# Moving block 0's first loads of the down product's weights in SyncE's queue

## The chip, the cores and the metric

The kernel runs on one core of one Trainium2 chip. A core has five engines that run side by side, each through its own queue of instructions in order: TensorE (PE: matrix products, with PEld for the loading of its stationary operand), VectorE (DVE), ScalarE (ACT), GpSimd (POOL) and SyncE (SP). SyncE computes nothing: it issues DMA transfers, which 16 DMA engines carry out. An instruction that has to wait holds up everything behind it in the queue of its engine. Intermediate results lie in the on-chip memory (SBUF) or in the banks of PSUM, where TensorE writes its products.

The metric is the time of one execution on the device, in microseconds (us): the median of several runs.

## The reference

One transformer block for 2048 rows of width 512, all in float32: a layer norm, attention with 32 heads of width 16 that share one key and one value, a residual, a second layer norm, a gated feed-forward product of inner width 1792, and another residual. Cut to what matters:

```python
q = (ln(x) @ wq) split into 32 heads of 16;  k = ln(x) @ wk;  v = ln(x) @ wv
p = softmax(q k^T / 4)
h = x + concat(p @ v) @ wo
out = h + (gelu(ln(h) @ w_gate) * (ln(h) @ w_up)) @ w_down
```

## The kernel before, in words

**Split numbers.** A product with float32 operands is made of three products of a faster format: an operand is split into a high and a low part (`split`), and high x high, high x low and low x high are summed. The weights of the feed-forward product are split once, by GpSimd (`part_weights`), and stored in two scratch tensors in HBM: `w1_d` (gate and up, 14 chunks of 128 columns) and `w2_d` (down, 14 chunks of 128 rows). From there they are loaded again for each block of rows: `load_w1` brings one chunk, 1 MB, into one of two buffers (L452), and `load_w2` brings two chunks, 1 MB, into one of three buffers (L457).

**Blocks and groups.** The 2048 rows are four blocks of 512 (b = 0 to 3). For a block, the heads are worked on in eight groups of four (g = 0 to 7), and for a group the 2048 keys in 16 chunks. For each chunk of keys TensorE makes the scores (L326), ScalarE takes the exponential (L330), and TensorE multiplies with the values and a column of ones and adds up in `acc` (L334). The loop counts half chunks: n runs through 256 of them for each block.

**The output of a group.** `evacuate` copies `acc` to `oT` (VectorE, L347), stores it to the scratch tensor `acc_d` (SyncE, L348) and reads it back in another arrangement into `oc` (four DMAs, L358). For each second group VectorE takes the reciprocals of the sums (L363), multiplies (L372) and splits the result into `o_hi` and `o_lo` (L108, L109).

**Two streams.** While the attention of block b + 1 runs, the rest of block b is computed between its pieces by the generator `dense(b)`: the product with wo (`pp`, L472), the residual with the input rows `xb` (loaded at L508, added at L535), the layer norm, the transposes (`pxt`, L543) into `x2h` and `x2l`, then for each of the 14 chunks f the products `pg` and `pu` (`up`), the gelu, and for each run of four chunks the product down (`down`, `pd`). `duo` (L472) makes two products at a time, each on one half of the rows of the array; between its two turns VectorE's one-column copies (L480) mark a bank as done. The last block's dense part has nothing beside it and runs as a tail.

**Who orders what.** The orders of TensorE, ScalarE and GpSimd are those of the program text everywhere (`manual_schedule`). Those of SyncE and VectorE are too, but only up to the end of the first part of the loop, the `while n < lead` loop, which ends three pieces of a group (16 half chunks) into block 1's attention. Behind it a planner in the framework orders SyncE and VectorE by its own estimate of when each instruction can run. It may also put one of these planned instructions between instructions of the written order, ahead of some that stand earlier in the text.

**Around the change.** At n = 256 the work on q and on the weights is finished, and the buffers of the dense part are opened in the place of theirs. At n = 260, within the written order, block 0's last group of heads is put out, and `dense(0)` is made and taken to its first `yield`: it issues the loads of `xb` for row tiles 0 and 1 and of the first two chunks of w1. The load of the next group's `qg` (L311) follows. The rest of `dense(0)` is taken in the planned part. In it the loads of w2 stand in the text in `for fs in RUNS`: the first two after the first `up`, the third and fourth behind the product down of the first run. `RUNS` is the 14 chunks as three runs of four and one of two.

Of the kernel before, what the change touches and what calls it, by code (L numbers as in the profile page):

```python
# [40 lines left out]
def kernel(  # L41
# [96 lines left out]
    def run(outer, first):  # L138
# [112 lines left out]
        def later_q():  # L251
            second = project_q(1, range(DC), nc.vector, 1)
            for _ in range(sum(RAMP.values())):
                yield next(second)

            next(q_rest)
            for _ in range(2 * DC - sum(RAMP.values())):
                yield next(second)
            yield from q_rest
            yield from second  # L260
            for b in range(2, NB):
                yield from project_q(b, range(DC), nc.vector, b)
            check_bound(eb, k2m)
# [77 lines left out]
        def take_out():  # L341
            for step in outs.pop(0):
                step()
# [106 lines left out]
        def load_w1(b, f):  # L450
            w = db.tile([P, 2, 2, DC, P], F32R, tag="w1", bufs=2, name=f"w1_{b}_{f}")
            nc.sync.dma_start(w.bitcast(F32), w1_d[f].bitcast(F32))  # L452
            return w[:, 0], w[:, 1]

        def load_w2(b, j):
            w = db.tile([P, 2, 2, D], F32R, tag="w2", bufs=3, name=f"w2_{b}_{j}")
            nc.sync.dma_start(  # L457
                w.bitcast(F32), w2_d[2 * j : 2 * j + 2].rearrange("f p i d -> p f i d").bitcast(F32)
            )
            return w[:, :, 0], w[:, :, 1]  # L460
# [38 lines left out]
        def dense(b, tail=False):  # L499
# [13 lines left out]
            xT_hi = db.tile([P, DC, T], F32R, tag="x2h", bufs=1, name=f"x2h_{b}")  # L513
            xT_lo = db.tile([P, DC, T], F32R, tag="x2l", bufs=1, name=f"x2l_{b}")
            w1 = {0: load_w1(b, 0), 1: load_w1(b, 1)}
            if b == 0:
                yield 0
            w2 = {}
            hs, xns, held = {}, {}, {}

            def project(t0):
# [94 lines left out]
            def up(f, gh, gl):  # L616
                hi, lo = w1.pop(f)
                terms = [
                    [
                        (wt[:, k, c, :], xt[:, c, :])  # L620
                        for c in range(DC)
                        for wt, xt in ((hi, xT_hi), (hi, xT_lo), (lo, xT_hi))
                    ]
                    for k in range(2)
                ]
                pg, pu = yield from product([f"pg_{b}_{f}", f"pu_{b}_{f}"], terms)
                g = db.tile([P, T], F32, tag="g", bufs=2, name=f"g_{b}_{f}")
                nc.vector.tensor_copy(g, pg)  # L628
                a = db.tile([P, T], F32, tag="ga", bufs=2, name=f"ga_{b}_{f}")
                nc.vector.tensor_tensor(a, g, g, op=ALU.mult)  # L630
                nc.vector.scalar_tensor_tensor(  # L631
                    a, a, 1.0 / GELU_A, g, op0=ALU.add, op1=ALU.mult
                )

                def gate():
                    nc.scalar.activation(a, a, AF.Tanh, scale=GELU_A * GELU_C)  # L636
                    nc.vector.scalar_tensor_tensor(a, a, 1.0, g, op0=ALU.add, op1=ALU.mult)
                    nc.vector.tensor_tensor(a, a, pu, op=ALU.mult)
                    split(nc.vector, gh[:, f % 2, :], gl[:, f % 2, :], a)

                gates.append(gate)
                if tail:
                    open_gates()
                yield CUT

            def down(fs, gs, last):
                tw = [w2.pop(f // 2) for f in fs[::2]]
                for t0 in range(0, TB, 2):  # L650
                    terms = []
                    for t in (t0, t0 + 1):
                        sl = slice(t * P, (t + 1) * P)
                        terms.append([
                            (gt[:, k, sl], wt[:, k, :])
                            for (gh, gl), (hi, lo) in zip(gs, tw)
                            for k in range(2)
                            for gt, wt in ((gh, hi), (gh, lo), (gl, hi))
                        ])
                    pds = yield from product(  # L660
                        [f"pd_{b}_{fs[0]}_{t0}", f"pd_{b}_{fs[0]}_{t0 + 1}"], terms
                    )
                    for t, pd in zip((t0, t0 + 1), pds):
                        nc.vector.tensor_tensor(hs[t], hs[t], pd, op=ALU.add)  # L664
                        if last:
                            nc.sync.dma_start(out_t[:, b * TB + t, :], hs[t])
                    yield CUT

            prev = None
            for fs in RUNS:  # L670

                early_f = 2 if fs is RUNS[-1] else 1
                gs = []
                for n, f in enumerate(fs):
                    if f % 2 == 0:
                        gs.append([
                            db.tile([P, 2, T], F32R, tag=tag, bufs=3, name=f"{tag}_{b}_{f}")
                            for tag in ("gh", "gl")
                        ])
                    yield from up(f, *gs[-1])  # L680
                    if f + 2 < FC:
                        w1[f + 2] = load_w1(b, f + 2)
                    if fs is RUNS[-1] and n == 0:
                        w2[f // 2] = load_w2(b, f // 2)
                    if n + 1 == early_f and prev is not None:
                        yield from down(*prev, False)
                    if fs is not RUNS[-1] and n + 1 == early_f:
                        for g in fs[::2]:
                            w2[g // 2] = load_w2(b, g // 2)
                prev = (fs, gs)  # L690
            yield from down(*prev, True)

# [19 lines left out]
        def drain():  # L712
            nonlocal work
            for _ in work or ():
                pass
            work = None
# [3 lines left out]
        def score(n):  # L720

            nonlocal acc
            i, u = divmod(n, 2)
            b, r = divmod(i, PER)
            g, kc = divmod(r, KC)
            if u == 0:
                if kc == 0:
                    cur["qg"] = qgs.pop((b, g))
                    acc = pss.tile([P, T], F32, tag="acc", bufs=1, name=f"acc_{b}_{g}")
                if kc == 2 and b * NG + g + 1 < NB * NG:  # L730
                    key = divmod(b * NG + g + 1, NG)
                    qgs[key] = load_q(*key)
                cur["p"] = sb.tile([P, 4, T], F32, tag="p", bufs=PB, name=f"p_{i}")
            scores(i, cur["p"], cur["qg"], kc, u)
            if u == 1:
                pend.append((b, g, kc, cur["p"], acc, n))
# [13 lines left out]
        with tc.manual_schedule(engines={mybir.EngineType.SP, mybir.EngineType.DVE}):  # L750
            parts = None
            if first:
                work = later_q()
                parts = part_weights(early.enter_context(tc.tile_pool(name="parts", bufs=1)))


            while n < lead:
                if n == 2 * PER:
                    drain()
                    for _ in parts or ():  # L760
                        pass
                    parts = None
                    early.close()
                    db = late.enter_context(tc.tile_pool(name="dense", bufs=1))
                if n % 4 == 0:
                    given = work is not None
                for _ in range(RAMP.get(n, n > 7 and n % 4 == 3) if given else 0):
                    if next(work, None) is None:
                        work = None
                score(n)  # L770
                n += 1
                if n % 4 == 2 and not given and len(pend) > 2:
                    finish(1)
                if n % 4:
                    continue
                if len(pend) > 2:
                    finish(len(pend) - 2)
                if outs:
                    take_out()
                if parts is not None and n > 12 and n % 24:  # L780
                    next(parts, None)
                if n == 2 * PER + 4:
                    primed = dense(0)
                    next(primed)
        assert not outs
        work = primed
        set_banks("ps_rest")
# [11 lines left out]
        for c in range(LEAD[0], (NB - 1) * NG * len(SIZES)):  # L799
            b, cb = divmod(c, NG * len(SIZES))  # L800
            cg = cb % len(SIZES)
            size, kind = SIZES[cg], None
            if b > 0 and cb == LEAD[b]:
                assert work is None
                work, todo = dense(b), list(kinds)
# [358 lines left out]
```

## Time and profile before

| | us |
|---|---|
| median of 3 runs | 1466.74 |
| lowest and highest | 1466.73, 1470.73 |
| the profiled execution | 1466.96 |
| its span, first to last instruction | 1465.2 |
| TensorE busy | 1417.1 |
| ScalarE busy | 1040.9 |
| VectorE busy | 533.3 |

The granted clock of TensorE was 0.997 of its full speed on average.

How to read the rows that follow. A row of a timeline has the start and the length in us, the engine, the line of the kernel, the operation, output and inputs by the program's names, and how many instructions were merged; a bracket tells how long the engine was idle ahead of it and what ended that. SPq is SyncE's queue; its DMA rows give the time that the issue took, not the transfer. A row of windows has the start and end of a stretch, its length, then the busy time of PE, PEld, DVE, ACT and POOL with the number of instructions, the granted clock, the mean busy share of the 16 DMA engines and the GB/s that they moved. A row of waits has the waiting engine and line, what it waited for, the sum, the number and the longest. A row of a tile has an instruction group's count, the shortest, median and longest duration in ns, and the starts of the first and the last in us.

### The profile page before, as it was taken

Reading aid. Unit: us, or ns where it says so; the run is one execution under the profiler, and the core shown is the slowest. Engines: PE = TensorE matmul, PEld = TensorE weight load, DVE = VectorE, ACT = ScalarE, POOL = GpSimd, SP = SyncE. Lnnn points to the kernel's source line nnn. Section 1 sums busy time; section 2 is a strip of 40 time slices with the busy share of each in tenths; the row PEclk is TensorE's granted clock in tenths of the full one; section 3 lists DMA queues with packets and bytes.
Section 4 is the critical chain, followed back from the end, with each engine's and each line's share of the span. In section 5 each row is a group of like instructions: output and inputs, shape, how many; then the busy total and the mean of one; then the engine's idle time right before and its main releaser. Section 6 shows DMA issues by size and latency. Waiting matters only on the chain.

```text
span 1465.2 us, 24785 instructions
## 1 busy us (share of the span) xinstructions
PE 1417.1 (97%) x10420; PEld 751.9 (51%) x10420; DVE 533.3 (36%) x920; ACT 1040.9 (71%) x1147; POOL 222.2 (15%) x301
## 2 busy tenths in 40 slices
PE   6999999999999999999999999999999999998998
PEld 5533333334555555554555555554555555556886
DVE  7413131213251424323251424324242423425665
ACT  7699999996777777776777777777777777762000
POOL 5477778620000000000000000000000000000000
PEclk9999999999999999999999999999999999999999
DMA  4465767661222332332132322321223313232551
GB/s 153 149 203 190 230 214 221 207 247 67 81 99 75 113 106 89 113 100 95 69 103 84 113 103 94 113 105 63 73 84 112 110 58 141 75 134 80 201 193 68
DMA packets 58864, 180.55 MB, mean 123 GB/s; under 512 B 8540, under 2 KB 8540, under 8 KB 51544
## 3 DMA queue, kind: packets, MB, share of 16 engines
q1 hardware_dynamic: 48912, 144.79, 28.9%
q0 software_dynamic: 9760, 34.08, 7.0%
q8 instruction: 84, 1.38, 0.4%
q14 instruction: 36, 0.29, 0.1%
q10 hardware_dynamic: 72, 0.00, 0.0%
HBM read 131.13 MB, written 47.71 MB: 122 GB/s over the span
## 4 chain that ended last, share of the span: by engine, by line
PE 76%; ACT 16%; issue 3%; DVE 2%; DMA 2%; SPq 0%; POOL 0%; ACTq 0%; POOLq 0%; DVEq 0%
PE acc L334 31%; PE s L326 16%; ACT p L330 15%; PE pd L472 5%; PE pu L472 5%; PE pg L472 4%; PE pq L177 3%; PE pg L494 3%; PE pd L494 3%; PE pu L494 3%; DMA acc_d<-oT 1%; PE pp L472 1%; PE pk L953 1%; PE pp L593 1%; DVE oc L363 1%
## 5 line engine op out<-in xcount | busy, mean ns | idle before, releaser
L330 ACT ACTIVATE p<-s 128x1024 f32<-128x1024 f32 x1024 | 969.5, 1041 | 271.1 <-PE s L326 270.5
L334 PE MATMUL acc<-p,v_sb 128*32 128x512 f32 x4096 | 492.5, 598 | 0.1
L326 PE MATMUL s<-qg,kaug 50*128 50x512 f32 x1984 | 395.6, 435 | 18.6 <-ACT p L330 13.9
L326 PEld LDWEIGHTS s<-qg,kaug 50*128 50x128 f32 x1984 | 172.3, 184 | 306.4 <-ACT p L330 192.4
L334 PEld LDWEIGHTS acc<-p,v_sb 128*32 128x32 f32 x4096 | 111.1, 109 | 243.3 <-issue 232.2
L472 PE MATMUL pu<-x2h,w 64*128 64x512 f32 x672 | 232.2, 392 | 1.6 <-DVE g L628 1.0
L472 PE MATMUL pg<-x2h,w 64*128 64x512 f32 x672 | 232.0, 392 | 0.8 <-DVE x2h L108 0.8
L117 POOL TENSOR_SCALAR rstd<-mv 128x1 f32<-128x1 f32 x16 | 3.5, 220 | 1017.1 <-DVE mv L115 1017.1
L472 PEld LDWEIGHTS pu<-x2h,w 64*128 64x128 f32 x672 | 124.8, 186 | 15.4 <-DVE g L628 2.2
L472 PE MATMUL pg<-x2l,w 64*128 64x512 f32 x336 | 132.0, 393 | 0.1
L472 PE MATMUL pu<-x2l,w 64*128 64x512 f32 x336 | 131.7, 392 | 0.0
L472 PEld LDWEIGHTS pg<-x2h,w 64*128 64x128 f32 x672 | 124.8, 186 | 12.3 <-DVE x2h L108 2.0
L472 PE MATMUL pd<-w,gh 64*128 64x512 f32 x672 | 105.4, 391 | 3.3 <-DVE mark_pd L480 3.3
L636 ACT ACTIVATE ga<-ga 128x512 f32<-128x512 f32 x56 | 36.2, 646 | 88.4 <-DVE ga L631 88.4
L628 DVE COPY g<-pg 128x512 f32<-128x512 f32 x56 | 38.7, 691 | 141.6 <-PE pg L472 134.4
L472 PEld LDWEIGHTS pd<-w,gh 64*128 64x128 f32 x672 | 63.4, 185 | 18.0 <-DVE mark_pd L480 3.7
L363 DVE RECIPROCAL oc<-oc 128x128 f32<-128x128 f32 x64 | 54.4, 911 | 47.7 <-DMA oc<-acc_d 47.7
L472 PE MATMUL pd<-w,gl 64*128 64x512 f32 x336 | 66.5, 392 | 0.0
L472 PEld LDWEIGHTS pg<-x2l,w 64*128 64x128 f32 x336 | 62.3, 185 | 8.0 <-DVE x2l L109 1.1
L472 PEld LDWEIGHTS pu<-x2l,w 64*128 64x128 f32 x336 | 62.3, 185 | 7.2
L480 DVE COPY mark_pu<-pu 128x1 f32<-128x1 f32 x42 | 6.6, 157 | 158.5 <-PE pu L472 158.5
L664 DVE TENSOR_TENSOR h<-h,pd 128x512 f32<-128x512 f32 x48 | 30.9, 683 | 91.4 <-PE pd L472 91.4
(224 smaller groups left out, 1322.8 us busy)
## 6 DMA issues: line engine op xcount, KB each, us to landing
w<-w_d SPq DMA_DIRECT2D x84, 1024.0 KB
qg<-q_d SPq DMA_DIRECT2D x62, 200.0 KB
q_d<-qh SPq DMA_DIRECT2D x32, 256.0 KB
acc_d<-oT SPq DMA_DIRECT2D x32, 256.0 KB
oc<-acc_d SPq DMA_DIRECT2D x128, 64.0 KB
w_d<-w_0b POOLq DMA_DIRECT2D x14, 512.0 KB, 5.4
w_d<-w_1b POOLq DMA_DIRECT2D x14, 512.0 KB, 3.7
x<-in_A_x_dram SPq DMA_DIRECT2D x16, 256.0 KB
```

What stands on the lines that cost most here:

```text
L177: nc.tensor.matmul(pq, wt[:, d, c * P : (c + 1) * P], xt[:, d, :], start=(n == 0), stop=(n == 3 * DC - 1),)
L326: nc.tensor.matmul(s[:, a, :], kaug[rows, kc * P : (kc + 1) * P], qg[rows, u, :], start=True, stop=True,)
L330: nc.scalar.activation(p[:, 2 * u : 2 * u + 2, :], s, AF.Exp, scale=SCALE)
L334: nc.tensor.matmul(acc[32 * j : 32 * j + 32, :], v_sb[:, kc, :], p[:, j, :], start=(kc == 0), stop=(kc == KC - 1), skip_group_check=True,)
L363: nc.vector.reciprocal(oc[:, 1, sl], oc[:, 1, sl])
L472: nc.tensor.matmul(banks[k], lhsT[rows], rhs[rows], start=(turn == 0 and i == 0), stop=(turn == 1 and i == n - 1), skip_group_check=True,)
L494: nc.tensor.matmul(bank, lhsT, rhs, start=(i == 0), stop=(i == len(ts) - 1))
L593: nc.tensor.matmul(pps[t], lhsT, rhs, start=start and i == 0, stop=stop and i == len(terms) - 1,)
L628: nc.vector.tensor_copy(g, pg)
L636: nc.scalar.activation(a, a, AF.Tanh, scale=GELU_A * GELU_C)
L664: nc.vector.tensor_tensor(hs[t], hs[t], pd, op=ALU.add)
L953: nc.tensor.matmul(pks[b], wt[:, c, :], xt[:, c, :], start=(c == 0 and n == 0), stop=(c == DC - 1 and n == 2),)
```

## The change

`dense(0)` gets a second stop: behind the loads of the first w1 it yields, and when taken up again it issues the first three loads of w2 (all that the three buffers hold) and yields once more. The loop up to `lead` takes that second step as its last act, still within the part in which SyncE follows the program text. So the loads have a written place in SyncE's queue, behind the output of block 0's last group of heads, the loads of `xb` and `w1`, and the load of the next `qg`. Where the loads stood before, `take_w2` now loads only what is not yet loaded. Blocks 1 to 3 load as before.

```diff
             w1 = {0: load_w1(b, 0), 1: load_w1(b, 1)}
+            w2 = {}
             if b == 0:
                 yield 0
-            w2 = {}
+
+                w2.update((j, load_w2(b, j)) for j in range(3))
+                yield 0
...
+            def take_w2(f):
+                if f // 2 not in w2:
+                    w2[f // 2] = load_w2(b, f // 2)
+
...
                     if fs is RUNS[-1] and n == 0:
-                        w2[f // 2] = load_w2(b, f // 2)
+                        take_w2(f)
...
                         for g in fs[::2]:
-                            w2[g // 2] = load_w2(b, g // 2)
+                            take_w2(g)
...
                 if n == 2 * PER + 4:
                     primed = dense(0)
                     next(primed)
+            next(primed)
```

## The prediction

> **What bounds the kernel now.** I read the first and fourth parts of the page first: the busy share of each engine and the chain that ended last.
>
> ```profile
> span 1465.2 us, 24785 instructions
> PE 1417.1 (97%) x10420; PEld 751.9 (51%) x10420; DVE 533.3 (36%) x920; ACT 1040.9 (71%) x1147; POOL 222.2 (15%) x301
> PE 76%; ACT 16%; issue 3%; DVE 2%; DMA 2%; SPq 0%; POOL 0%; ACTq 0%; POOLq 0%; DVEq 0%
> ```
>
> TensorE is busy for 97% of the span and holds 76% of the chain. It is idle for 1465.2 - 1417.1 = 48.1 us in the whole run. SyncE's queue has 0% of the chain: its 84 weight loads are not what the end waits for. So a change on SyncE can do something only where a transfer that it delays or hurries stands in front of TensorE. I therefore read the timeline of SyncE's queue around the change next.
>
> ```profile
> 294.81 1.54 SPq L311 DMA_DIRECT2D qg<-q_d  x2
> 307.20 1.42 SPq L457 DMA_DIRECT2D w<-w_d  x3
> 316.37 0.34 SPq L348 DMA_DIRECT2D acc_d<-oT  x1
> 319.05 1.72 SPq L358 DMA_DIRECT2D oc<-acc_d  x4
> 320.81 0.90 SPq L508 DMA_DIRECT2D xb<-in_A_x_dram  x2
> 321.75 0.91 SPq L452 DMA_DIRECT2D w<-w_d  x2
> 322.75 0.71 SPq L311 DMA_DIRECT2D qg<-q_d  x2
> 340.70 0.95 SPq L508 DMA_DIRECT2D xb<-in_A_x_dram  x2
> 351.49 0.35 SPq L348 DMA_DIRECT2D acc_d<-oT  x1
> 353.58 1.71 SPq L358 DMA_DIRECT2D oc<-acc_d  x4
> ```
>
> L457 is the load of w2. All three loads that the change touches stand at 307.20, ahead of the output of block 0's last group of heads (L348 at 316.37, read back by L358 at 319.05). In program order they come after the load of qg at 322.75, and from there to 340.70 SyncE issues nothing. The same stretch, cut by the traffic on the DMA engines (last two columns: share and GB/s):
>
> ```profile
> 308.00:318.00 10.00, 10.00 (x68) 3.02 (x64) 0.69 (x1) 10.00 (x12) 0.00 (x0) 1.00 0.91 341
> 318.00:320.00 2.00, 2.00 (x14) 0.53 (x12) 0.00 (x0) 2.00 (x4) 0.00 (x0) 1.00 0.02 8
> 320.00:332.00 12.00, 11.24 (x82) 5.14 (x80) 5.26 (x8) 11.80 (x14) 0.00 (x0) 1.00 0.77 274
> 332.00:340.00 8.00, 8.00 (x68) 3.98 (x67) 0.12 (x2) 5.21 (x6) 0.00 (x0) 1.00 0.01 2
> 340.00:346.00 6.00, 6.00 (x52) 2.91 (x50) 3.77 (x8) 3.94 (x5) 1.73 (x4) 1.00 0.24 87
> 314.00:316.00 2.00, 2.00 (x16) 0.61 (x14) 0.35 (x1) 2.00 (x4) 0.00 (x0) 1.00 1.05 426
> ```
>
> 308 to 318 holds 10 x 341 = 3.41 MB: w2 (3 x 1.05 MB) and the 0.26 MB of acc_d. In full flow it moves at 426 GB/s. 320 to 332 holds what oc, xb, the first two w1 and qg bring, 3.29 MB. 332 to 340 is empty. 340 to 346 holds 0.52 MB, the next two xb.
>
> **The change, part by part.**
>
> (1) The three loads leave 307.20. In front of them SyncE's queue held one wait, for POOL's last store of a split weight:
>
> ```profile
> SPq L457 <- DMA w_d<-w213b: 4.2, 1, 4.2
> ```
>
> Nothing was queued behind that wait that could have gone (the output at 316.37 waits for VectorE's copy of 315.65, below), so taking it away is worth 0. POOL's queue has no more work from there to the layer norms of block 0 and nothing of it is passed.
>
> (2) What they were ahead of: the output and its way back. The store took from 316.37 to the issue at 319.05, 2.68 us, with the end of w2 still moving; in the next group, alone, 353.58 - 351.49 = 2.09. So o_hi and o_lo can come 0 to 0.6 us sooner; I take 0.6, from the nearer row. Is TensorE waiting for them? The timelines of VectorE and TensorE:
>
> ```profile
> 315.65 0.69 DVE L347 COPY oT<-acc 128x512 f32<-128x512 f32 x1 [28.12 <-PE acc L334]
> 322.70 3.39 DVE L363 RECIPROCAL oc<-oc 128x128 f32<-128x128 f32 x4 [6.36 <-DMA oc<-acc_d]
> 327.31 0.69 DVE L109 TENSOR_TENSOR o_lo<-oc,o_hi 128x512 fp32r<-128x512 f32 x1
> 327.84 0.50 PE L326 MATMUL s<-qg,kaug 50*128 50x512 f32 x2 [0.42 <-ACT p L330]
> 328.41 0.40 PE L472 MATMUL pp<-wo_lo,o_hi 64*128 64x512 f32 x2
> 328.64 0.40 PE L472 MATMUL pp<-wo_hi,o_lo 64*128 64x512 f32 x2
> ```
>
> o_lo is done at 328.00 and first read at 328.64. Ahead of that stands a score at 327.84 that waited for ScalarE's exponential, not for o. ScalarE's work hides the 0.6 us entirely: worth 0 (bounds 0 and -0.6). Were o late instead, the cover is 0.64 us and every further microsecond would cost TensorE one.
>
> (3) Where they go: behind qg, issued from about 323.5. Three issues take 1.42 us on SyncE, inside its pause to 340.70: 0. Their wait for POOL's stores is long over. Data: the queue ahead of them is drained at 332, and 3.15 MB at 426 GB/s take 7.4 us, so they land at about 339.5, in the empty stretch. A slower bound: at the 274 GB/s of 320 to 332 they need 11.5 us, to 343.5.
>
> The Trainium skill, "DMA: Bandwidth & Descriptors", section "Where 436 GB/s comes from", says that between HBM and the on-chip memory the memory's share of about 358 GB/s per core binds. By it w2 would take 8.8 us and land near 341; the row of 426 GB/s does not bear that out, and the measurement decides.
>
> (4) What is late next. First the transfers behind w2 on the queue: xb of row tiles 2 and 3, issued at 340.70. Their consumers:
>
> ```profile
> 355.01 1.29 DVE L535 TENSOR_TENSOR h<-pp,xb 128x512 f32<-128x512 f32 x2 [3.54 <-PE pp L472]
> 360.80 0.55 DVE L120 TENSOR_SCALAR xn<-h,mv,rstd 128x512 f32<-128x512 f32 x1 [0.98 <-POOL rstd L118]
> 364.58 1.09 PE L543 MATMUL pxt<-ident,xn 128*128 128x128 f32 x8
> ```
>
> They are due at 355.0, and even the slower bound leaves 355.0 - 343.5 = 11.5 us for 0.52 MB. Then 364.58 - 361.35 = 3.2 us lie between the last xn and its transposes. Second, w2 itself, first read by pd:
>
> ```profile
> L472 PE MATMUL pd<-w,gh x672: 383/391/496, 438.0 to 1337.8; 64*128 64x512 f32 x168
> ```
>
> 438.0 is 94 us after the later landing: 0. Third, w1 and qg keep their place ahead of w2.
>
> (5) The traffic now falls on a stretch in which TensorE, not ScalarE, sets the pace. Does traffic slow its products? Two rows of the same product, to set beside 328.41 and 328.64 (in a full window) from the empty window 332 to 340:
>
> ```profile
> 336.62 0.40 PE L472 MATMUL pp<-wo_lo,o_hi 64*128 64x512 f32 x2
> 336.85 0.39 PE L472 MATMUL pp<-wo_hi,o_lo 64*128 64x512 f32 x2
> ```
>
> 0.23 us from one pair to the next in both: 0.
>
> (6) The order of the rest. Behind the lead-in, SyncE's and VectorE's orders are the planner's, made from its own times, and w2's place is one of its inputs. What a new order may be worth must be bounded from stretches that show two of them; the interval between the outputs of the first groups of two successive blocks, cut into windows:
>
> ```profile
> 351.49:691.33 339.84, 333.37 (x2686) 175.95 (x2682) 120.00 (x207) 251.50 (x272) 4.06 (x10) 1.00 0.28 96
> 691.33:1026.07 334.74, 329.59 (x2658) 173.02 (x2656) 115.79 (x199) 250.27 (x271) 3.28 (x8) 1.00 0.27 94
> 404.90 3.39 DVE L363 RECIPROCAL oc<-oc 128x128 f32<-128x128 f32 x4 [0.64 <-DMA oc<-acc_d]
> 409.39 0.68 DVE L628 COPY g<-pg 128x512 f32<-128x512 f32 x1
> 410.13 0.50 PE L472 MATMUL pu<-x2h,w 64*128 64x512 f32 x1 [0.62 <-DVE g L628]
> 1336.80 0.73 PE L472 MATMUL pd<-w,gh 64*128 64x512 f32 x4 [3.31 <-DVE mark_pd L480]
> ```
>
> The first interval is 5.1 us longer, but 3.8 of it is more TensorE work (28 matmuls more). Idle: 339.84 - 333.37 = 6.47 us against 5.15. So block 0 has 1.3 us to win by an order as good as the next one's. The dearest wait for VectorE in the rows of TensorE is the 3.31 us at 1336.80, in the tail: the most that one misplaced VectorE step is seen to cost; I take 0, since TensorE's, ScalarE's and POOL's orders are written out and VectorE's steps follow when those release them.
>
> **The sum.** 0 (wait) + 0 (output, hidden) + 0 (issue) + 0 (landing) + 0 (traffic) + 0 (order). The profiled execution took 1466.96 us, its span of 1465.2 and 1.8 around it, 0.2 above the median of 1466.74. I forecast 1466.7 for the median. Its own range: the 1.3 us of idle time and 0.6 of part 2 downward, one stall of 3.3 us upward: 1464.8 to 1470.0.
>
> **Rivals.**
>
> A, slower: VectorE's new order in block 0. When the heads' reciprocals (3.39 us in the rows of 322.70 and 404.90) stand ahead of the copy or the mark that frees a PSUM bank, TensorE waits. At 410.13 this costs 0.62 us: the copy of g came at 409.39, behind them. It happens once for each pair of groups, four times in block 0. Priced with the dearest such wait, 3.31 each, one is within 0.3% and two decide: 1466.7 + 6.6 = 1473.3. For it: VectorE's order is not written out there, and the reciprocals wait for a DMA that shares its engines with the loads. Against it: from 366 on the loads of w2 are over in both kernels, and no interval above shows it.
>
> B, faster: the order gets better. Equal to the second interval's idle time it gives 1465.4, which is within 0.3%; only if nearly all of 6.47 us vanished, 1460.2, would it be faster. Against it: both intervals keep more than 5 us.
>
> C, slower by the queue: xb of tiles 2 and 3 wait behind w2. Worked out from rows: TensorE loses time when xb lands after 355.0 + 3.2 = 358.2. These 0.52 MB, issued at 340.70, are over by 346, 5.3 us, so w2 would have to flow past 352.9, 20.9 us after 332, at 151 GB/s or less. At 100 GB/s it ends at 363.5, xb 5.2 later at 368.7, and the run 10.5 later at 1477.2. The rows give 426 and 274. The Trainium skill, "DMA: Bandwidth & Descriptors", section "Queues, rings and completion order", has each engine consume a ring's descriptors in order, which is this rival's ground; what the queue holds is short enough here that the order costs nothing.
>
> D: nothing moves, because the planner may set the loads early again. Both the outputs and the loads are then under the same written order, so this has hardly a chance, and its time is 1466.7 too.
>
> **How the numbers follow.** 0.3% is 4.4 us, about what a measurement of this kernel can tell from no change. The likeliest, transfers hidden before and after, with small shifts of order: 0.71, D among them. A 0.16 and C 0.03, slower 0.19 together. B in full 0.10, as the rows leave little to win, but a whole new order for two queues is not seen in this profile. The range must hold 8 in 10: the likeliest case and the nearer half of A, up to two stalls, and a little below for B: 1464.0 to 1473.3.
>
> **What would show it.** Step 1: SyncE's rows have no w2 near 307 and three behind qg near 323.5. Step 2: the window 308 to 318 is nearly empty, acc_d to oc takes about 2.1 us, pp still starts near 328.2. Step 3: 332 to 340 is full, at about 400 GB/s. Step 4: h at 355.0, pg at 366.6, pd at 438.0 as before. Step 5: pairs of pp 0.23 apart. Step 6: the first interval again 339.8, idle 6.5. I am wrong if pp or pg moves by more than 1 us, or if that interval moves by more than 3 us: then the order of VectorE or SyncE in it, compared row by row, is where it went.

## The result: slower by two parts in a thousand

The changed kernel took 1470.29 us (median; 1467.18 to 1476.44), the kernel before, measured beside it, 1466.89 (1464.31 to 1473.05). The ratio is 1.0022, with a 95% interval of 1.0011 to 1.0032. So in this comparison the changed kernel was slower by 3.4 us, which is less than the 0.3% that I had named as what a measurement can tell from no change, but more than this comparison's own uncertainty. I had forecast no change.

The profiled execution of the changed kernel took 1469.37 us. From the page of its profile, the span, the engines' busy times and the shares of the chain of work that ended last:

```profile
span 1467.7 us, 24786 instructions
PE 1419.1 (97%) x10420; PEld 752.9 (51%) x10420; DVE 535.3 (36%) x920; ACT 1040.8 (71%) x1147; POOL 222.4 (15%) x301
PE 76%; ACT 16%; issue 3%; DVE 2%; DMA 1%; POOL 1%; SPq 0%; ACTq 0%; POOLq 0%; DVEq 0%
```

The span is 2.5 us longer, and TensorE is busy 2.0 us longer (1417.1 before) with the same 10420 products. That is the first thing to see: most of the loss is not waiting. The same products took longer.

**The place of the change.** The timeline of SyncE's queue in the changed kernel:

```profile
315.11 0.35 SPq L348 DMA_DIRECT2D acc_d<-oT  x1
317.21 1.91 SPq L358 DMA_DIRECT2D oc<-acc_d  x4
319.50 0.84 SPq L508 DMA_DIRECT2D xb<-in_A_x_dram  x2
320.39 0.90 SPq L452 DMA_DIRECT2D w<-w_d  x2
321.39 0.72 SPq L311 DMA_DIRECT2D qg<-q_d  x2
322.15 3.70 SPq L457 DMA_DIRECT2D w<-w_d  x3
339.44 0.95 SPq L508 DMA_DIRECT2D xb<-in_A_x_dram  x2
350.24 0.35 SPq L348 DMA_DIRECT2D acc_d<-oT  x1
```

The three loads (L457) went where the change puts them. From one output to the next, 315.11 to 350.24, it takes 35.13 us; before it took 351.49 - 316.37 = 35.12. The whole stretch in which loads were moved costs nothing here. The order of instructions on TensorE, VectorE, ScalarE and GpSimd is the same in both kernels from the first to the last; SyncE's differs in the place of these three loads alone.

**Where the time went.** The intervals between outputs (L348) of the changed kernel as windows: block 0's dense part, block 1's, a longer stretch of blocks 1 and 2, and the tail.

```profile
350.24:691.47 341.23, 334.10 (x2686) 176.49 (x2682) 119.91 (x207) 251.76 (x272) 4.06 (x10) 1.00 0.29 95
691.47:1026.38 334.91, 329.82 (x2658) 173.55 (x2656) 115.90 (x199) 250.38 (x271) 3.27 (x8) 1.00 0.28 94
734.84:1317.71 582.87, 574.20 (x4660) 303.90 (x4658) 201.65 (x343) 437.32 (x473) 3.95 (x9) 1.00 0.29 98
1317.71:1467.70 149.99, 138.34 (x600) 110.76 (x600) 87.05 (x140) 16.20 (x26) 3.12 (x8) 0.96 0.39 134
```

The last two of them in the kernel before:

```profile
734.69:1317.22 582.53, 573.85 (x4660) 303.32 (x4658) 201.56 (x343) 437.15 (x473) 3.95 (x9) 1.00 0.28 98
1317.22:1465.20 147.98, 136.59 (x600) 110.03 (x600) 87.11 (x140) 16.31 (x26) 3.11 (x8) 0.97 0.39 136
```

The first interval grew by 341.23 - 339.84 = 1.39 us, the second by 0.17, the rest up to the tail by 0.18, the tail by 2.01, and what lies ahead of 315.11 shrank by 1.26. The surprise is the third row. Hundreds of microseconds behind the change, with the same 4660 products in the same order, TensorE is busy 574.20 instead of 573.85 us. As the order is the same there, I asked whether one kind of product had become longer, and set the groups of products of each shape side by side. TensorE's groups of `pd` in the tail, which ran after 1355 us, in the kernel before (count, busy us, mean ns of one, idle ahead):

```profile
L494 PE MATMUL pd<-w,gh 128*128 128x512 f32 x112 | 34.5, 389 | 0.0
L494 PE MATMUL pd<-w,gl 128*128 128x512 f32 x56 | 21.8, 389 | 0.0
```

The same groups in the changed kernel:

```profile
L494 PE MATMUL pd<-w,gh 128*128 128x512 f32 x112 | 35.1, 395 | 0.0
L494 PE MATMUL pd<-w,gl 128*128 128x512 f32 x56 | 22.1, 394 | 0.0
```

389 became 395 ns for the one product that reads w2, and no other group of products behind 1355 us moved: `pg` and `pu` stay at 389 to 390 ns. From start to start, which is what back-to-back products cost, the trace gives 226.74 ns before and 232.46 after, and 168 x 5.72 ns = 0.96 us.

The change does not touch these products. But it asks for w2's buffers at an earlier point of the program, and buffers are laid out in the order in which they are first asked for. The layout of the dense part's buffers in the two built programs, as byte in each partition and the rest after division by 256:

```
        w2 (moving operand of pd)    gh, gl (stationary operands of pd)
before  126208, rest 0               93440, rest 0;   105728, rest 0
after    80768, rest 128             118016, rest 0;  130304, rest 0
```

### The profile page after: what moved, and what is told of

Same layout as the page of the kernel before. It is cut to its first block, busy times and chain, and to the rows that moved or that the text cites. A ratio compares the mean times of both kernels' runs of the same rounds, so it can differ in the third digit from the quotient of the medians.

```text
span 1467.7 us, 24786 instructions
## 1 busy us (share of the span) xinstructions
PE 1419.1 (97%) x10420; PEld 752.9 (51%) x10420; DVE 535.3 (36%) x920; ACT 1040.8 (71%) x1147; POOL 222.4 (15%) x301
## 4 chain that ended last, share of the span: by engine, by line
PE 76%; ACT 16%; issue 3%; DVE 2%; DMA 1%; POOL 1%; SPq 0%; ACTq 0%; POOLq 0%; DVEq 0%
PE acc L334 31%; PE s L326 17%; ACT p L330 15%; PE pu L472 5%; PE pd L472 5%; PE pq L177 3%; PE pg L472 3%; PE pd L494 3%; PE pg L494 3%; PE pu L494 3%; PE pp L472 1%; DMA acc_d<-oT 1%; PE pp L596 1%; PE pxt L546 1%; DVE oc L363 0%
## 5 line engine op out<-in xcount | busy, mean ns | idle before, releaser
L334 PEld LDWEIGHTS acc<-p,v_sb 128*32 128x32 f32 x4096 | 111.1, 109 | 243.5 <-issue 232.4
L472 PEld LDWEIGHTS pg<-x2h,w 64*128 64x128 f32 x672 | 124.7, 186 | 11.8 <-DVE x2h L108 2.0
```

Of the source, the lines that this page charges most:

```text
L334: nc.tensor.matmul(acc[32 * j : 32 * j + 32, :], v_sb[:, kc, :], p[:, j, :], start=(kc == 0), stop=(kc == KC - 1), skip_group_check=True,)
L472: nc.tensor.matmul(banks[k], lhsT[rows], rhs[rows], start=(turn == 0 and i == 0), stop=(turn == 1 and i == n - 1), skip_group_check=True,)
```

## Theories

Address: w2 now begins 128 bytes beside a multiple of 256, its partners `gh` and `gl` on one, and `pd` pays for that. Worth 0.96 us in the tail, about 0.35 in the two blocks between 735 and 1317, and by my estimate half of that, about 0.2, in block 0: 1.5 us. Order: the place of the loads in SyncE's queue, or what it does to the return of `oc`, costs the rest or all. Scatter: what exceeds 1.5 us is the difference between two sets of runs. The first interval and the tail both hold waits that differ from run to run.

## Experiments

**The two kernels again, and two other places for the loads.** `again_before` and `again_after` repeat the kernels. In `written_early` the loads are written ahead of the output:

```diff
+                    early_w2.update((j, load_w2(0, j)) for j in range(3))
...
-                w2.update((j, load_w2(b, j)) for j in range(3))
-                yield 0
+                w2.update(early_w2)
...
-            next(primed)
```

In `behind_outputs_ahead_of_w1` they stand behind the output but are the first of `dense(0)`:

```diff
+            w2 = {}
+            if b == 0:
+                w2.update((j, load_w2(b, j)) for j in range(3))
             if not tail:
                 load_x(0)
...
-                w2.update((j, load_w2(b, j)) for j in range(3))
-                yield 0
...
-            next(primed)
```

The expectations of these four know only Order, as "theory P", and Scatter, as "theory C". Address came after them: in the next set it is "theory L", and Order is "theory O".

> The kernel before, timed as if it were a change: the ratio that no change gives. Both theories: 0.999 to 1.001. If it differs from 1 by as much as 0.002, the measured 0.22 per cent of the change is no more than the noise of this kernel. Its trace gives a second sample of the waits for oc and of the tail's clock.

> The changed kernel once more, for a second trace. Theory P (the place of the three loads costs 3 us): slower than before by 2 to 5 us, and the loss is found again in the same stretches of block 0, where the reciprocals wait for their DMA (561 to 605 and 646 to 691, 2.4 us together in the first trace). Theory C (the stretch around the change costs nothing; the difference is TensorE's granted clock in the tail and the latency of single DMAs, which vary from run to run): the waits for the DMA stand in other groups this time, and the times follow the mean granted clock.

> The three loads are issued by the program text as soon as their buffers are open, ahead of the output of block 0's last group: SyncE's order is that of the kernel before, but written. Theory P: equal to before (1466 to 1468). Theory C: the same as the changed kernel and before alike, within the scatter of either; it cannot be told by the place.

> The three loads stand directly behind the output and its way back, ahead of xb, w1 and qg. Theory P, if being behind the outputs is what costs: as slow as the changed kernel (1469 to 1472). If instead the place behind w1 and qg costs: equal to before. Theory C: within 2 us of either, with h of tiles 0 and 1 at 340 at the latest as before, since xb then lands about 7.4 us later than its 324, still ahead of 340.

Measured, all against the kernel before on the same chip: `again_before` 0.9996 [0.9981, 1.0011], `again_after` 1.0002 [0.9986, 1.0018], `written_early` 1.0000 [0.9984, 1.0016], `behind_outputs_ahead_of_w1` 0.9999 [0.9982, 1.0016]. Here the 0.22% was not to be seen, not even for the changed kernel itself, so these times decide nothing; the rows do. The 2 to 5 us that theory P had forecast did not come. In `written_early` the order of every engine is that of before, but w2 lies at 43904, 128 beside a multiple. Its group of `pd` in the tail:

```profile
L495 PE MATMUL pd<-w,gh 128*128 128x512 f32 x112 | 35.1, 395 | 0.0
```

So 395 ns come without the changed order, which leaves the addresses. And the stretch between the two outputs around the loads took 35.13, 35.13, 35.12 and 35.11 us in the four: the loads may stand ahead of the output, behind it, ahead of `xb` and w1 or behind `qg`, and it costs the same.

**Order and address crossed.** To calm the return of `oc`, four kernels put two more empty steps between the outputs and the reciprocals (they also state the drain of VectorE's work a little earlier in the tail's text, which changed no order there). Two have the order of before, two that of the change; in each pair one has w2 on a multiple of 256 and one 128 beside it, by tiles of 128 bytes around w2:

```diff
-                outs.extend([[], []])
+                outs.extend([[], [], [], []])
```

```diff
+            if not pads:
+                pads.append(db.tile([P, 32], F32, tag="pad0", bufs=1, name="pad0"))
+                nc.gpsimd.memset(pads[0][:, :1], 0.0)
             w = db.tile([P, 2, 2, D], F32R, tag="w2", bufs=3, name=f"w2_{b}_{j}")
...
```

> The kernel before with two more empty steps between the reading back of a pair of groups and its reciprocals, in the written part only, so that VectorE no longer stands before a late DMA there while TensorE waits for q. It is the base of the next three. Both theories: the interval between the outputs at 254 and 288 loses its scatter of 32.4 to 38.8 us and stays near 32 to 33; times 1464 to 1468. From the output near 316 to the one near 1317: 1000.8 as in both traces of the kernel before.

> The changed kernel with the same two empty steps. Theory O (the order of the three loads costs) and theory L (the change moves w2's buffers in the on-chip memory from a multiple of 256 bytes to 128 beside one, and every later load of w2 is slower for it): both 1001.7 to 1002.6 for the interval from 316 to 1317, the last pair of block 0 at 45.2 instead of 44.3, and 1 to 2 us slower than the one before. Theory C (chance only): no difference to the spaced kernel before.

> The order of the kernel before, but a pad of 128 bytes ahead of w2's buffers and one behind, so that they start 128 bytes beside a multiple of 256 as in the changed kernel. Theory L: 1001.7 to 1002.6 for the interval from 316 to 1317, the last pair of block 0 at 45.2, from the output near 735 to the one near 1317 582.8. Theory O: 1000.8, 44.3 and 582.5.

> The order of the changed kernel, but a pad of 128 bytes puts w2's buffers back to a multiple of 256. Theory L: 1000.8, 44.3 and 582.5 as in the kernel before. Theory O: 1001.7 to 1002.6 and 45.2.

| order of the loads | w2 on a multiple of 256 | w2 128 beside |
|---|---|---|
| before | 1467.99 us, 0.9993 [0.9976, 1.0009] | 1469.56 us, 1.0002 [0.9986, 1.0019] |
| changed | 1466.92 us, 0.9986 [0.9970, 1.0002] | 1468.46 us, 0.9991 [0.9975, 1.0008] |

By the medians the 128 bytes cost 1.57 us in the one order and 1.54 in the other. The changed order is not seen to cost anything in either column; its medians are 1.1 us lower in both. The interval from the output at 735 to that at 1317 is 582.43 and 582.48 on a multiple, 582.79 and 582.93 beside it. What I had expected of block 0's last group of heads failed: it does not go with the address. It took 45.6 and 45.7 us with w2 on a multiple, where I had expected 44.3. What I had expected of the whole stretch from the output at 316 to that at 1317 failed with it: it took 1000.8 and 1002.0 us with w2 on a multiple, 1001.1 and 1001.6 beside it. Block 0's waits differ by more than the address costs there.

**w2 put back, in the changed kernel as it is.** `w2_realigned` is the changed kernel with the same small tiles, w2 at 80896. Its order of loads is the changed one.

> The changed kernel with one edit: a tile of 128 bytes is laid out ahead of w2, so that w2 begins at byte 80896 of each partition, a multiple of 256, in place of 80768. Order of the loads as changed. Theory address (the 128 bytes cost, the order costs nothing): the products of pd in the tail come back from 395 to 389 ns (226.7 ns from start to start), the interval from the output at about 735 to the one at about 1317 from 582.8 to 582.5, and the time lies at that of the kernel before, within 0.1%. Rival place (what counts is where in the memory w2 lies, 80 KB against 126 KB, or what lies beside it): 395 ns stay. Rival order (it is the place in SyncE's queue that costs): the time stays 0.2% above the kernel before, whatever the products take.

It took 1466.95 us against 1467.12, a ratio of 0.9997 [0.9983, 1.0011]. Its group in the tail:

```profile
L501 PE MATMUL pd<-w,gh 128*128 128x512 f32 x112 | 34.5, 389 | 0.0
```

The long interval took 582.55 us. Both went back with the 128 bytes, so neither the region of the memory nor the order is what `pd` pays for.

**Both operands moved.** Is it the moving operand's own address, or its distance from the stationary one? In `w2_and_gh_shifted` w2 stays where the change puts it, 128 beside, and a tile of 128 bytes ahead of `gh` moves `gh` and `gl` beside a multiple as well:

```diff
+                        if not pads:
+                            pads.append(db.tile([P, 32], F32, tag="pad0", bufs=1, name="pad0"))
+                            nc.gpsimd.memset(pads[0][:, :1], 0.0)
```

> The changed kernel with the tiles of gh and gl, the stationary operands of pd, moved by 128 bytes as well: w2, gh and gl all lie 128 beside a multiple of 256. Theory moving operand alone: pd in the tail stays at 395 ns and the interval 735 to 1317 at 582.8. Rival, the two operands against each other (they collide when one is 128 off the other): pd returns to 389 ns and the interval to 582.5. Rival, each on its own: the weight loads of pd get longer too, and pd goes above 395 ns.

```profile
L495 PE MATMUL pd<-w,gh 128*128 128x512 f32 x112 | 34.4, 389 | 0.0
L495 PE MATMUL pd<-w,gl 128*128 128x512 f32 x56 | 21.8, 389 | 0.0
```

389 ns again, and 582.63 us for the long interval; this was one execution, and the same kernel is timed further down. So it is the distance between the two operands: 128 bytes apart (after division by 256) is slow, the same rest is quick, whichever rest it is. This also fits `pg` and `pu`, whose operands `x2h` (48000) and w1 (64384) both lie 128 beside a multiple: they run at 389 ns in both kernels.

The fourth combination, the moving operand on a multiple and the stationary one 128 beside, stands in the kernel before itself, in the products for q at its start. Their weights (`wq_hi`, from 93056) lie 128 beside a multiple; the rows `xT_hi` lie on one for block 0 (138496) and 128 beside for block 1 (43904). The second product and the last but one of an unbroken row of 15 for block 0, then the second and the last of a row of 6 for block 1:

```profile
48.60 0.39 PE L177 MATMUL pq<-xT_lo,wq_hi 128*128 128x512 f32 x1
51.39 0.40 PE L177 MATMUL pq<-xT_lo,wq_hi 128*128 128x512 f32 x1
54.07 0.39 PE L177 MATMUL pq<-xT_lo,wq_hi 128*128 128x512 f32 x1
54.98 0.39 PE L177 MATMUL pq<-xT_hi,wq_lo 128*128 128x512 f32 x1
```

Twelve steps take 2.79 us, 232.5 ns each; four steps take 0.91 us, 227 ns each. So the slow time comes with the distance in this direction too. Equal rests do not always give the quick time, though. Two more rows of 6 for block 1 begin with steps of 231 to 233 ns and end at 226 and 227, and where the products for q run in threes between pieces of attention, with both operands 128 beside a multiple, the step from the second to the third took 226 to 240 ns in the same profile. Steady it is in the long rows of the tail.

The Trainium skill, "TensorE: Matmul & The Clock Gate", section "Step-by-step: what each phase is for", has two independent read ports, one for the streaming operand and one for the weights, and says: "Loading the next tile's weights doesn't steal SBUF read bandwidth from the running matmul." By that the distance would be worth nothing. The rows of 389 and 395 ns disagree, and the measurement decides. That the two reads meet is what the pattern suggests, but no run here shows it.

**How much would the queue bear?** `six_mb_more_behind_w2` puts six copies of 1.05 MB from HBM to HBM (of scratch weights, read by nobody) behind the three loads, to try the cover of step 4:

```diff
+                for j in range(6):
+                    nc.sync.dma_start(w3_d[j].bitcast(F32), w1_d[j].bitcast(F32))
```

> The changed kernel with six copies of 1.05 MB from device memory to device memory (of scratch weights that nobody reads afterwards) written behind the three loads of w2 on SyncE's queue, ahead of the xb of row tiles 2 and 3. Tests the cover of 11.5 us that step 4 took. Step 4 and rival C: the xb must land by 358.2; six copies at 200 to 420 GB/s, counted as they are read, end 15 to 31 us after about 343, at 358 to 374, so h of row tiles 2 and 3 waits for a DMA and TensorE loses the part beyond 358.2, 0 to about 16 us, and the outputs behind shift by as much. If instead the copies run beside the xb without holding it up, h stands at its place (4.8 us after the output at about 350) and nothing moves: then the order on the queue isn't what the xb would wait for, and rival C was never to be had at any rate.

From its timelines of SyncE and VectorE, and the window from one output to the next:

```profile
325.23 10.73 SPq L523 DMA_DIRECT2D w_d<-w_d  x6
339.34 1.19 SPq L509 DMA_DIRECT2D xb<-in_A_x_dram  x2
359.12 1.29 DVE L541 TENSOR_TENSOR h<-pp,xb 128x512 f32<-128x512 f32 x2 [9.02 <-DMA xb<-in_A_x_dram]
350.13:398.79 48.66, 46.35 (x328) 23.24 (x326) 15.07 (x27) 31.13 (x34) 1.56 (x4) 0.93 0.36 117
```

The same two readings in the changed kernel:

```profile
353.75 1.29 DVE L538 TENSOR_TENSOR h<-pp,xb 128x512 f32<-128x512 f32 x2 [3.54 <-PE pp L472]
350.24:394.50 44.26, 43.35 (x328) 21.43 (x326) 15.07 (x27) 31.03 (x34) 1.56 (x4) 1.00 0.21 70
```

In this one execution `xb` was issued at 339.34 and arrived only at 359.1: the copies hold it up. Whether by their place in the queue or by sharing the DMA engines, these rows do not tell. `h` moved by 5.4 us, and the group took 48.66 - 44.26 = 4.40 us longer, of which 3.0 are longer products (46.35 - 43.35, at a granted clock of 0.93). So rival C's loss can be had, with 6.3 MB more in the queue. The change alone stays clear of it, as `h` there still waits for TensorE and not for `xb`.

**A version against both.** `before_with_tail_mark` is the kernel before with the wider spacing of the outputs, and with VectorE's mark for `pd` in the tail between its two pairs of layer norms, by a written order:

```diff
...
+        last = dense(NB - 1, True)
+        with tc.manual_schedule(engines={mybir.EngineType.DVE}):
+            for said in last:
+                if said == HOLD:
+                    for step in work:
+                        if step == CUT:
+                            break
+                elif said == EDGE:
+                    drain()
+                    break
```

> A version against both kernels: the kernel before (w2 on a multiple of 256, loads ahead of the output), with the outputs of the groups one step further apart in the written order, and with VectorE's marks for pd in the tail put between the two pairs of layer norms. Theory: the 3.3 us in which TensorE waits for the mark at 1336.8 go, and with them the drop of the granted clock behind it (0.6 to 0.8 between 1335 and 1345); the tail from the last output to the end, 148.0 to 150.0 us, becomes 144 to 146, and the time falls by 2 to 4 us, 0.1 to 0.3%. Rival: the wait only moves to the second pair of norms, and the time stays within 0.1%.

It took 1468.72 us against 1467.12, a ratio of 1.0013 [0.9994, 1.0032]: nothing gained, where I had forecast 2 to 4 us. TensorE's waits around the place:

```profile
PE pxt L543 <- DVE h L667: 2.4, 1, 2.4
PE pd L472 <- DVE mark_pd L480: 0.6, 1, 0.6
```

The single wait of 3.3 us became one of 0.6 and one of 2.4, as the rival had it.

**Once more on one chip.** The changed kernel, its two variants without the distance of 128 bytes, and the kernel before, as controls beside each other.

> The changed kernel again. Theory address: pd in the tail at 395 ns, the interval from the output at about 735 to that at about 1317 at 582.8 to 583.0, and the median 1.2 to 1.8 us (0.08 to 0.12%) above those of the two kernels below that have the same order of loads but no 128 bytes between the operands. Rival order: level with them, and all three above the kernel before by 2 us or more.

> The changed kernel with w2 moved by 128 bytes onto a multiple of 256, again. Theory address: level with the kernel before within 0.1%; 389 ns; 582.4 to 582.6. Rival order: 0.15 to 0.2% above the kernel before.

> The changed kernel with gh and gl moved by 128 bytes, so that they lie as w2 does. Theory of the distance between the operands (both 128 beside is as good as both on a multiple): level with the realigned kernel within 0.05%, 389 ns. If the 128 bytes of the moving operand cost by themselves: level with the changed kernel.

> The kernel before against itself: ratio 1.000 within 0.15%, which is the scatter of the comparison. In block 0's last group of heads, output at about 647, the reciprocals start 9.6 us behind the output if that belongs to the kernel, and 10.5 or more if it belongs to the run.

| kernel | us | ratio to before (1467.24 us) | tail `pd`, ns | 735 to 1317, us |
|---|---|---|---|---|
| changed | 1470.11 | 1.0016 [1.0000, 1.0031] | 395 | 582.89 |
| changed, w2 realigned | 1468.32 | 1.0004 [0.9988, 1.0021] | 389 | 582.46 |
| changed, gh and gl shifted too | 1468.35 | 1.0006 [0.9991, 1.0022] | 389 | 582.59 |
| before | 1467.96 | 0.9999 [0.9983, 1.0016] | 389 | 582.48 |

The changed kernel stands 1.8 us above its two variants, and these 0.4 us above the kernel before's own repetition. Intervals of 0.15% to either side do not prove 0.12%. Four pairs of medians that differ in the distance and ran on one chip (1.57, 1.54, 1.79, 1.76, the last two against the same runs of the changed kernel) agree with the 1.5 us worked out from the rows; a fifth, `written_early` against `again_before`, gave -0.3, so whole times alone would not carry it. The rows do. In all 18 profiles of this study the mean of `pd` from start to start in the tail is 226.7 ns (ten without the distance) or 232.5 (eight with it), with nothing between 226.8 and 232.4, and the long interval sorts the same way: 582.43 to 582.66 us and 582.70 to 582.99.

The last kernel also settles the first interval. Windows of the kernel before, profiled once more: block 0's dense part, its last group of heads, and the tail.

```profile
350.23:692.44 342.21, 335.06 (x2686) 177.02 (x2682) 119.80 (x207) 251.64 (x272) 4.05 (x10) 1.00 0.28 95
644.44:692.44 48.00, 44.62 (x346) 23.92 (x342) 18.16 (x35) 31.83 (x34) 2.49 (x6) 0.96 0.34 110
1318.30:1465.60 147.30, 135.37 (x600) 108.70 (x600) 86.94 (x140) 16.27 (x26) 3.10 (x8) 0.99 0.39 137
```

The unchanged kernel took 342.21 us here and 339.84 in its first profile, with the same order: 2.4 us, more than the 1.39 that I had to explain. The difference sits in the last group, where `oc` came back later (the reciprocals start 11.8 us behind the output instead of 9.6) and TensorE then waited 1.6 us for VectorE's `h`. The changed kernel's other two profiles took 340.5 and 339.8 us. So this part of the loss can come from the run without the change. The tail's part beyond 0.96 us probably does too: behind TensorE's wait of 3.3 us for the mark, present in both kernels, the granted clock drops in some runs and not in others. Windows behind it in the changed kernel:

```profile
1335.00:1340.00 5.00, 2.68 (x12) 1.83 (x12) 0.73 (x6) 1.88 (x3) 1.54 (x4) 0.61 0.00 0
1340.00:1345.00 5.00, 4.00 (x19) 3.03 (x17) 3.95 (x6) 3.11 (x6) 0.00 (x0) 0.70 0.67 207
```

The same windows of the kernel before, in the profile beside the prediction:

```profile
1335.00:1340.00 5.00, 3.20 (x19) 2.37 (x20) 1.67 (x5) 1.92 (x3) 1.32 (x3) 0.82 0.01 1
1340.00:1345.00 5.00, 4.09 (x19) 3.20 (x18) 2.70 (x4) 3.99 (x8) 0.00 (x0) 0.84 0.86 316
```

And in the repetition of the kernel before:

```profile
1335.00:1340.00 5.00, 2.10 (x16) 1.47 (x16) 1.72 (x8) 2.33 (x3) 1.53 (x4) 1.00 0.00 0
1340.00:1345.00 5.00, 3.77 (x21) 2.59 (x20) 3.39 (x6) 4.32 (x8) 0.00 (x0) 1.00 0.86 263
```

0.61 and 0.70, 0.82 and 0.84, 1.00 and 1.00, with a tail of 149.99, 147.98 and 147.30 us. The changed kernel as it stands had 149.5 to 150.0 us in three profiles and the kernel before 147.3 to 148.1 in three, which alone would look like the kernel. But `w2_realigned`, with the changed order, had 148.4 in one profile and 150.6 in the other, and over all 18 profiles the mean tail with the distance is 0.9 us longer than without it, which is no more than the 0.96 (single tails took 146.9 to 150.7). The Trainium skill, "TensorE: Matmul & The Clock Gate", section "What's actually happening", has the clock halved after at least one idle window of about 3.4 us, and the window free-running. The wait here is just short of that, and no run shows where a window began, so whether this rule makes the difference between the runs stays open.

## Why the prediction was wrong

(1), the wait in front of the loads, and (2), the output's way back: right. From `acc_d` to `oc` it took 317.21 - 315.11 = 2.10 us, as foretold; `o_lo` came 0.3 us sooner behind the output than before, and that was hidden. My reading of the cover was wrong, however. I took 328.64 for the first read of this group's o, and so 0.64 us for the cover. `pp` takes the four chunks of o one after the other, and only the last of them is this group's; it is read from 330.73 on, and its `o_lo` first at 331.42, 3.4 us after it was done. The kernel before, profiled once more, shows it: its output stands at 315.11, and it came back late.

```profile
320.48 1.72 SPq L358 DMA_DIRECT2D oc<-acc_d  x4
328.73 0.69 DVE L109 TENSOR_TENSOR o_lo<-oc,o_hi 128x512 fp32r<-128x512 f32 x1
327.39 0.39 PE L472 MATMUL pp<-wo_hi,o_lo 64*128 64x512 f32 x2
```

`o_lo` was done 14.3 us behind the output there instead of 11.6, after products on `o_lo` had begun, and the stretch from output to output still took 35.12 us. The 0 of this step was right, with more room than I gave it.

(3), issue and landing: the cost of 0 was right. The mean rate of the transfer was below the row of 426 GB/s that I took. The windows of the changed kernel that answer to those of before:

```profile
308.00:318.00 10.00, 10.00 (x70) 2.73 (x62) 0.69 (x1) 10.00 (x13) 0.00 (x0) 1.00 0.08 28
320.00:332.00 12.00, 11.24 (x84) 5.22 (x86) 5.36 (x8) 11.80 (x14) 0.00 (x0) 1.00 0.93 287
332.00:340.00 8.00, 8.00 (x74) 3.99 (x67) 1.27 (x3) 5.19 (x6) 0.00 (x0) 1.00 0.95 329
340.00:346.00 6.00, 5.84 (x50) 3.17 (x42) 2.51 (x7) 3.96 (x5) 1.73 (x4) 1.00 0.33 112
```

The empty stretch filled with 329 GB/s, between my two rates of 274 and 426, and w2 ended at about 341, between 339.5 and the bound of 343.5: from 316 to 341 the DMA engines moved 6.7 MB, which is all that had been issued up to w2. TensorE's busy time in the two windows full of loads is what it was (11.24 of 12, 8.00 of 8). The 358 GB/s that I had set aside, with a landing near 341, were nearer than my 426.

(4) is the step that failed, in its second point: "w2 itself, first read by pd ... 438.0 is 94 us after the later landing: 0." I priced when w2 arrives and not where. The first point, `xb`, was right: `h` still waits for TensorE, and it takes the six copies to change that. But the same w2, at another address, makes each `pd` of the tail 5.7 ns longer, 0.96 us there and about 1.5 in all, in a part of the program that I held to be out of reach. The sum had no term for it, and no rival had it as a mechanism; the chance of 0.19 for slower was all A and C.

(5), traffic against products: right. (6), the order of the rest: 0 was right, and rivals A and B are out, as the orders are the same instruction by instruction. My reason for 0 (VectorE's steps follow when those release them) was not what was tested, since the planner found no new order.

Of the 3.4 us of the first comparison 1.5 are accounted for by the rows (0.96 and 0.35 read from them, 0.2 estimated). The other 1.9 are 0.13%, and the three comparisons of the changed kernel gave 1.0022, 1.0002 and 1.0016. That they are scatter is likely from the run-to-run rows above but not shown one by one; what the realigned kernels leave for the order is -0.17% to +0.21% (the ends of their intervals). Why 128 bytes between two operands cost TensorE anything is open too; of the distances only 0 and 128 were compared.

## What to carry to other kernels

An edit that moves the first use of a buffer moves addresses, and with them the price of instructions far from the edit. So compare the mean time of each form of product, before and after, ahead of looking for waits: TensorE busy longer with the same number of products is a sign of it (a lower granted clock is another cause). When a kernel keeps TensorE busy for 97% of its span, try the moving and the stationary operand of a product with the same rest modulo 256 bytes; here it was worth 1.5 us of 1467. For effects of 0.1%, an interval between two events that the trace repeats to 0.1 us says more than the times of whole runs.

## What the runs showed of the hardware that was not expected

- In the long rows of the tail, a 128x512 product of split numbers took 226.7 ns from start to start when its operands' addresses in a partition had the same rest modulo 256 (both 0 or both 128), and 232.5 when they were 128 apart. A long row for q, with the distance the other way, took 232.5 too. In short rows it took 226 to 240 at equal rests. In pairs of products on half the rows each, the difference was far smaller: 0.35 us over the two blocks between 735 and 1317.
- The same wait of 3.3 us left the granted clock at 1.00 in one run and at 0.61 and 0.70 in another, over the window of 5 us in which it ended and the next.
- One store and read-back through HBM (`acc_d` to `oc`), 2.1 us when alone, took 5.2 to 7.2 us over the 18 profiles in block 0's last group, behind a load of 1 MB issued 3.4 us earlier; in three profiles of the kernel before it took 5.2, 5.6 and 7.1.
